# A Fourier-convolution layer with a feed-forward part: first forward stage on 64x64 tiles over two PSUM banks, kernel units finished in pairs, a rebuilt handover and a new order

## The chip, the cores and the metric

The kernel runs on one core of a Trainium2 chip. The metric is the device time in microseconds of one execution; the runs are given with their median. PE is the matrix engine (PEld its weight loads), DVE the vector engine, ACT the scalar engine, POOL the GpSimd engine, SP the engine that issues DMAs. All compute engines run their own instruction streams in order and wait for each other through semaphores.

## The reference

```python
x = A_u                                             # 1 x 2048 x 512
sa, ca, ga, sb, cb, gb = (silu(c) @ w_mod) in six   # each 512 wide
h = layernorm(x) * (1 + ca) + sa
x = x + ga * A(h)
h = layernorm(x) * (1 + cb) + sb
x = x + gb * B(h)

def A(u):          # per channel d of 512, N = 128 complex modes, L = 2048
    K[d, l] = real(sum_n C[d, n] * exp(dt * A[d, n] * l) * dt * B[d, n])
    y = causal convolution of u[:, d] with K[d]     # by FFT of length 2 L
    return y + u * Dskip

def B(x):          # F = 1792
    return relu(x @ w1 + b1) ** 2 @ w2 + b2
```

All data are 32-bit floats.

## The kernel before

Two parts follow each other. The first computes the convolution by a Fourier transform written as matmuls; the second is the feed-forward part, whose matmuls run on values split into a high and a low half (type fp32r).

**The convolution.** The 512 channels are taken in `NC` = 8 blocks of 64, lettered A to H. Sequence positions are split into 32 x 64 points. For a block, `u_pieces` transforms the input: four calls of `stage1` (each: 4 groups of 4 channels, 8 matmuls with 64 columns of data as weights and 128 moving columns of the constant `d1_sb`, into one PSUM bank, and one ACT copy), then four calls of `stage2` (16 matmuls against the table `t2_sb`), copied by ACT. Its fourth piece also copies the halves of the spectrum crosswise by two DMAs (`sws`, `sw`). `d1_sb` is block diagonal in four blocks of 32 rows and columns.

The kernel K is computed in `NU` = 32 units of 16 channels. For unit u, POOL makes the phases (`kgen_phase`, L729) and amplitudes (`kgen_amp`, L749, L753), ACT the sines (L739 to L741), DVE their products (`kgen_rl`, L763 to L766), and PE sums over the modes with 128x32 tiles (`kgen_mm`, L773) into one half of the bank `kg`. `finish(u)` then copies that half to `ksb` (ACT L836), adds the skip term (DVE L837) and calls `stage1` on it. `product_pieces(c)` (letters a to h) runs `stage2` on the block's kernel spectrum, multiplies it on DVE with the input's (L783), and transforms back in a first step (L792, four blocks of 16 matmuls, copied by DVE, L798).

PSUM has eight banks: a ring `ps` of three for stage1, stage2 and L792, one bank `kg`, and four (`tg`) for the sines. The amplitudes lie in a ring of three buffers in `rtl` and `llph`, so POOL's amplitude of unit u waits until PE has used that of unit u - 3.

**What sets the order.** The strings of `ORDER` say which pieces are traced between units u and u + 1 (r rows of the first layernorm, x exponentials, l late modulation, A to H and a to g as above). `keep_order` then reorders: it simulates all engines with the durations of `weight` and takes, per engine, the ready group with the longest way to the end (`urgent` adds to it). The resulting order of each engine is fixed before the run.

**The handover.** The last block's product (`last`) is traced by hand, not by `ORDER`. Meanwhile w1 is split into halves (ACT L897, POOL L918) and w2 partly (ACT L893, POOL L894); `inverse(n)`, n = 0 to 3 (L946, 32x32 tiles, 128 matmuls each into the four `accs` banks), makes the second step of the back transform for a quarter of the rows, which DVE (n = 0) or ACT (L955) evacuates and POOL adds to the input (L958). Four rows of 128 at a time are then normalised: `statistics(s)`, `prepare(s)` (norm on DVE L973, the scaled bias b2 added to x on POOL L975, four transposes L979, scale and shift on ACT L986 and, for s < 4 and q > 1, DVE L982; cast on ACT L990, low half `h0l` on POOL L992).

**The feed-forward part.** 56 rounds of `ffn1` (12 matmuls of 128x512, L1040 to L1043) and `ffn2` (12, L1060 to L1062), PE alone being full. Here PE runs 1344 such matmuls, whatever comes before.

Of the kernel before, what the change touches and what calls it, by code (L numbers as in the profile page):

```python
# [36 lines left out]
NC = 512 // NCH  # L37
# [3 lines left out]
    "rxrrrrrrrrrrrrrrrABAAABDAlAA..DBBA.BD.BDaDBaaDaCCa..xaBaaC.C.CbbDbbCEECb."  # L41
    ".CEbE.b.bcccc.Dcxc..c.HcEEdxdddEdE..G.ddH.deeeeFFH.eHGFFeF..FGFFe.GeGHffGHffGfGf."
    ".H..ff.gg.ggH.gg.gg"
# [58 lines left out]

def weight(ins):
# [3 lines left out]
    if "DMA" in type(ins).__name__:  # L107
# [10 lines left out]
            if cols == 32 and ins.ins[1].ap[0][1] == 32:  # L118
                return 42, 42 + 200
            tiles = 128 // cols if cols in (32, 64, 128) else 1  # L120
# [21 lines left out]
def keep_order(tc, traced, slots, in_turn, whole, urgent):  # L142
# [101 lines left out]
    for _ in groups:  # L244
# [7 lines left out]
        if e == "PE":  # L252
            kind = free_size(groups[g][0].ins[1]) if len(groups[g][0].ins) > 1 else shape
# [38 lines left out]
def tile_adaln_ssm_ffn(  # L292
# [41 lines left out]
    PS, XY = 3, 7  # L334
# [180 lines left out]
    urgent = {}  # L515
# [7 lines left out]
    hurry(mark, 125781)  # L523
# [7 lines left out]
    hurry(mark, 150000)  # L531
# [45 lines left out]
    gs4, g4, s4 = (ctile(n, [P, 128]) for n in ("gs4", "g4", "s4"))  # L577
# [12 lines left out]
    hurry(mark, -13262)  # L590
# [3 lines left out]
    def row_pieces():  # L594
        for s, row in enumerate(rows):
# [10 lines left out]
            hurry(mark, 150000)  # L606
# [11 lines left out]
    def late_modulation():  # L618
        for wm, v in ((wm_sb, sbc), (wm_cb, cbc)):
            m = bank("ps", PS)  # L620
            mod_rows(wm, m)
            mt = ring(kp, "mt", 1, [P, 128])
# [11 lines left out]
    def stage1(src, dst, o):  # L634

        ps = bank("ps", PS)
        for i in range(4):
            for r in range(2):
                nc.tensor.matmul(  # L639
                    ps[64 * r : 64 * r + 64, 128 * i : 128 * i + 128], src[:, i], d1_sb[:, r], start=True, stop=True)  # L640
        nc.scalar.copy(dst[:, o // 4], ps.rearrange("p (t m) -> p m t", t=4))  # L641
# [24 lines left out]
    def u_pieces(c):  # L666
        xs = xus[c] = spectrum()
        for g in range(4):
            stage1(x_sb[c][:, 4 * g : 4 * g + 4], xs, 4 * g)
            yield  # L670
        for g in range(4):
            nc.scalar.copy(piece(xs, g), stage2(xs, g))
            if g == 3:
                sw = sws[c] = spectrum()
                for h in range(2):
                    nc.sync.dma_start(sw[64 * h : 64 * h + 64], xs[64 - 64 * h : 128 - 64 * h])
            yield

# [144 lines left out]
    work.update((chr(97 + c), product_pieces(c)) for c in range(NC - 1))  # L823
# [4 lines left out]
    def finish(u):  # L828

        c = u // 4  # L830
        if u % 4 == 0:
            xks[c] = spectrum()
        kps = kg[:, u % 2]
        kgen_mm(kq.pop(u), kps)
        ksb = ring(kp, "ksb", 2, [P, 4, 64])
        nc.scalar.copy(ksb, kps)  # L836
# [296 lines left out]
```

## Time and profile before

| what | value |
|---|---|
| median of 3 runs | 651.43 us (649.11 to 651.5) |
| the profiled execution | 646.92 us |
| its span | 645.1 us |
| PE, DVE, ACT, POOL busy | 584.7, 384.0, 342.2, 302.7 us |
| mean granted clock of PE | 0.984 |

In a row of instruction groups stand the line, engine, operation, the tiles (out<-in), the shapes, the count, then busy time, mean ns of one, and the idle time just before with what ended it. A 32-bit matmul of the code is two records in the trace. In rows of groups by line and shape, `128*64` is the tile of PE in rows and columns of the array. The digits of the page are busy tenths in 40 slices of 16.1 us.

### The profile page before, as it was taken

The page shows a single profiled execution, that of the slowest core. Times are in us where ns is not written, and L with a number is a line of the kernel's source. Part 1 is how long each engine was busy: PE and PEld are TensorE (multiplying, and loading weights), DVE is VectorE, ACT ScalarE, POOL GpSimd, SP SyncE. Part 2 cuts the span into 40 slices and gives each one's busy share as a digit, 9 for nine tenths or more (in the row PEclk, how much of TensorE's full clock was granted, in tenths as well). Part 3 has the DMA queues.
Part 4 walks back from the last instruction along what each step waited for, and adds up shares of the span by engine and source line. Part 5 has one row for each costly group of instructions (what it writes and reads, how often), then busy time and mean ns, then how long its engine had stood idle before and what let it go on. Part 6 is the DMA issues. An engine that isn't in the chain of part 4 may idle for free.

```text
span 645.1 us, 20810 instructions
## 1 busy us (share of the span) xinstructions
PE 584.7 (91%) x9314; PEld 507.1 (79%) x9314; DVE 384.0 (60%) x655; ACT 342.2 (53%) x632; POOL 302.7 (47%) x243
## 2 busy tenths in 40 slices
PE   1367998999899999987899999999999999999995
PEld 1265997899799998885668888888888888888884
DVE  6999956899799778744659532533325333252223
ACT  5963888989887977361645532244322433222220
POOL 5696799889999887158969300011000100000000
PEclk9999999999999999998799999999999999999998
DMA  9942030311331233465222000100001000010001
GB/s 324 381 133 68 3 69 4 68 36 38 69 70 39 82 69 86 139 206 201 85 83 73 28 0 1 65 1 0 1 1 66 1 1 1 0 66 0 1 1 65
DMA packets 21705, 42.30 MB, mean 66 GB/s; under 512 B 3696, under 2 KB 9200, under 8 KB 20336
## 3 DMA queue, kind: packets, MB, share of 16 engines
q1 hardware_dynamic: 21184, 40.84, 20.8%
q8 instruction: 73, 1.20, 0.8%
q10 hardware_dynamic: 432, 0.14, 0.1%
q14 instruction: 16, 0.13, 0.1%
HBM read 28.39 MB, written 4.19 MB: 51 GB/s over the span
## 4 chain that ended last, share of the span: by engine, by line
PE 71%; DVE 11%; POOL 7%; issue 5%; ACT 4%; DMA 2%; DVEq 0%; SPq 0%; POOLq 0%; ACTq 0%
PE tg L1060 8%; PE tg L1062 8%; PE tg L1061 8%; PE ps L1040 6%; PE ps L1041 6%; PE ps L1043 6%; PE ps L649 6%; PE ps L792 6%; PE ps L639 5%; PE kg L773 3%; PE kg L1040 2%; PE kg L1041 2%; PE kg L1043 2%; ACT tables L720 2%; DVE xy L598 2%
## 5 line engine op out<-in xcount | busy, mean ns | idle before, releaser
L1048 DVE TENSOR_TENSOR xy<-xy 128x512 f32<-128x512 f32 x56 | 44.6, 796 | 157.8 <-ACT rw L1047 106.2
L1046 ACT ACTIVATE xy<-ps,b1c 128x512 f32<-128x512 f32 x42 | 28.9, 688 | 129.7 <-PE ps L1043 129.7
L975 POOL TENSOR_TENSOR big<-big,lo 128x512 f32<-128x512 f32 x16 | 21.6, 1355 | 152.9 <-DVE xy L973 152.5
L649 PE MATMUL ps<-xy,t_sb 128*64 128x64 f32 x2048 | 67.1, 223 | 1.8 <-DVE xy L783 0.9
L649 PEld LDWEIGHTS ps<-xy,t_sb 128*64 128x64 f32 x2048 | 63.9, 138 | 3.8 <-issue 1.1
L792 PE MATMUL ps<-e_sb,xy 128*64 128x128 f32 x1024 | 61.3, 274 | 4.7 <-ACT xy L641 1.9
L792 PEld LDWEIGHTS ps<-e_sb,xy 128*64 128x64 f32 x1024 | 56.0, 139 | 6.3 <-ACT xy L641 2.3
L641 ACT COPY xy<-ps 128x512 f32<-128x512 f32 x64 | 36.8, 589 | 11.8 <-PE ps L639 10.1
L753 POOL TENSOR_TENSOR rtl<-tables 128x1024 f32<-128x1024 f32 x22 | 43.0, 1955 | 0.1
L783 DVE TENSOR_TENSOR xy<-ps,xy 128x512 f32<-128x512 f32 x64 | 40.0, 683 | 2.0 <-PE ps L649 1.7
L798 DVE COPY big<-ps 128x256 f32<-128x256 f32 x64 | 24.2, 419 | 20.3 <-PE ps L792 20.0
L729 POOL TENSOR_TENSOR llph<-lo,big 128x1024 int32<-128x1024 int32 x16 | 34.3, 2141 | 3.8 <-ACT tg L741 2.3
L1040 PE MATMUL ps<-h0h,w1h 128*128 128x512 f32 x88 | 35.8, 407 | 0.0
L729 POOL TENSOR_TENSOR rtl<-lo,big 128x1024 int32<-128x1024 int32 x16 | 34.3, 2141 | 2.8 <-ACT tg L741 2.1
L639 PE MATMUL ps<-d_sb,ksb 128*64 128x128 f32 x512 | 33.2, 274 | 1.1 <-DVE ksb L837 0.6
L639 PE MATMUL ps<-d_sb,big 128*64 128x128 f32 x512 | 31.4, 274 | 0.8 <-ACT big L605 0.7
L1040 PE MATMUL ps<-h,w1h 128*128 128x512 f32 x80 | 31.4, 393 | 0.0
L1046 ACT ACTIVATE xy<-kg,b1c 128x512 f32<-128x512 f32 x14 | 9.6, 689 | 39.4 <-PE kg L1043 39.4
L1049 DVE TENSOR_TENSOR rw<-xy,rw 128x512 fp32r<-128x512 f32 x37 | 28.5, 770 | 2.9
L639 PEld LDWEIGHTS ps<-d_sb,ksb 128*64 128x64 f32 x512 | 28.0, 137 | 2.3 <-DVE ksb L837 1.0
L639 PEld LDWEIGHTS ps<-d_sb,big 128*64 128x64 f32 x512 | 27.9, 137 | 2.0 <-ACT big L605 1.0
L773 PE MATMUL kg<-rtl 128*32 128x64 f32 x1408 | 25.6, 221 | 4.1 <-issue 4.1
(247 smaller groups left out, 1574.0 us busy)
## 6 DMA issues: line engine op xcount, KB each, us to landing
xy<-xt SPq DMA_DIRECT2D x32, 256.0 KB, 5.2
xy<-xy SPq DMA_DIRECT2D x16, 512.0 KB, 6.1
xy<-w_mod SPq DMA_DIRECT2D x6, 1024.0 KB, 8.6
out_dram<-xy SPq DMA_DIRECT2D x16, 256.0 KB, 2.1
xy<-w SPq DMA_DIRECT2D x14, 256.0 KB, 2.7
raw<-w SPq DMA_DIRECT2D x6, 512.0 KB, 5.4
t_sb<-c_t SPq DMA_DIRECT2D x1, 2048.0 KB, 16.9
i2c<-c_i SPq DMA_DIRECT2D x1, 2048.0 KB, 8.7
```

Of the source, the lines that this page charges most:

```text
L639: nc.tensor.matmul(ps[64 * r : 64 * r + 64, 128 * i : 128 * i + 128], src[:, i], d1_sb[:, r], start=True, stop=True)
L649: nc.tensor.matmul(ps[64 * r : 64 * r + 64, 64 * i : 64 * i + 64].rearrange("p (h q t) -> p q h t", h=2, t=2), t2_sb[:, 8 * g + i, r], src ...
L729: nc.gpsimd.tensor_tensor(ph.rearrange("p d r (a b) -> p (d r) a b", a=4), bc(low_phase[:, us].rearrange("p d r b -> p (d r) b"), 2, 4), b ...
L773: nc.tensor.matmul(kps[32 * q : 32 * q + 32, d, :], am[:, r, 4 * q + d, 64:96], am[:, r, 4 * q + d, 0:64], start=(r == 0), stop=(r == 1))
L792: nc.tensor.matmul(ps[64 * m : 64 * m + 64, 128 * i : 128 * i + 128], pairs(y)[:, g, i // 2, 64 * m : 64 * m + 64, i % 2], e1_sb[:, h], st ...
L1040: pe.append(nc.tensor.matmul(ps, w1h[:, q, fs], hh[:, q, :], start=(q == 0), stop=False))
L1041: pe.append(nc.tensor.matmul(ps, wl[:, q], hh[:, q, :], start=False, stop=False))
L1043: pe.append(nc.tensor.matmul(ps, w1h[:, q, fs], hl[:, q, :], start=False, stop=(q == 3)))
L1048: nc.vector.tensor_mul(rr, rr, rr)
L1060: pe.append(nc.tensor.matmul(acc, r2l[:, ms], hi_, start=(t == 0), stop=False))
L1061: pe.append(nc.tensor.matmul(acc, r2h[:, ms], lo_, start=False, stop=False))
L1062: pe.append(nc.tensor.matmul(acc, r2h[:, ms], hi_, start=False, stop=(t == NF - 1)))
```

## The change

Five things change.

1. `stage1` takes 8 groups a call instead of 4, as 32 matmuls on 64x64 tiles: the upper and the lower 64 rows of the data go to two row halves of the array, each with its half of `d1_sb` (the blocks that are zero are left out), and write to two banks, which ACT copies one after the other. The matmul count of stage 1 doubles, the moving columns halve.
2. `finish` copies two units at once from the whole `kg` bank and calls `stage1` once for both.
3. The crosswise DMAs become pieces of their own (digits in `ORDER`), and the last block's product a lettered piece (h).
4. The handover: `inverse(n)` alternates between the `tg` banks and the `ps` and `kg` banks, and inverses 0 and 1 stand in a fixed turn on PE; for s < 4 the norm runs on ACT instead of DVE, three of four scale-and-shift steps on DVE instead of two, and the scaled bias is made and added after the inverses.
5. `ORDER`, the `hurry` values and the planner's PE costs are new. A few small tiles (`gs4`, `g4`, `s4`, `mt`) move into buffers that are free by then.

```diff
+def shape_of(ins):
+    return free_size(ins.ins[1]) + 1000 * (ins.ins[1].ap[0][1] == 64)
...
+            if cols == 64 and rows == 64:
+                return 30, 30 + 170
...
-    hurry(mark, 125781)
+    hurry(mark, 107010)
...
-        hurry(mark, 7656)
+        hurry(mark, 36379)
...
     def stage1(src, dst, o):
 
-        ps = bank("ps", PS)
-        for i in range(4):
-            for r in range(2):
-                nc.tensor.matmul(
-                    ps[64 * r : 64 * r + 64, 128 * i : 128 * i + 128], src[:, i], d1_sb[:, r], start=True, stop=True)
-        nc.scalar.copy(dst[:, o // 4], ps.rearrange("p (t m) -> p m t", t=4))
+        banks = [bank("ps", PS) for _ in range(2)]
+        for i in range(8):
+            for r, h in ((0, 0), (1, 1), (1, 0), (0, 1)):
+                hs = slice(64 * h, 64 * h + 64)
+                m = nc.tensor.matmul(
+                    banks[h][64 * r : 64 * r + 64, 64 * i : 64 * i + 64], src[hs, i], d1_sb[hs, r, hs], start=True, stop=True)
+                whole[m.ins.name] = banks[0].tensor.name
+        for h, ps in enumerate(banks):
+            nc.scalar.copy(dst[:, 2 * o : 2 * o + 2, 64 * h : 64 * h + 64], ps.rearrange("p (d t m) -> p d m t", d=2, t=4))
...
+    def swap_piece(c):
+        xs, sw = xus[c], spectrum()
+        sws[c] = sw
+        for h in range(2):
+            nc.sync.dma_start(sw[64 * h : 64 * h + 64], xs[64 - 64 * h : 128 - 64 * h])
+        yield
...
     def finish(u):
 
-        c = u // 4
-        if u % 4 == 0:
+        kgen_mm(kq.pop(u), kg[:, u % 2])
+        if u % 2 == 0:
+            return
+        c, o = u // 4, u // 2 % 2
+        if o == 0:
             xks[c] = spectrum()
-        kps = kg[:, u % 2]
-        kgen_mm(kq.pop(u), kps)
-        ksb = ring(kp, "ksb", 2, [P, 4, 64])
-        nc.scalar.copy(ksb, kps)
-        nc.vector.tensor_add(ksb[:, :, 63], kps[:, :, 63], ds4[:, 4 * u : 4 * u + 4])
-        stage1(ksb, xks[c], 4 * (u % 4))
+        ksb = ring(kp, "ksb", KSB, [P, 8, 64])
+        both = kg.rearrange("p u d x -> p (u d) x")
+        nc.scalar.copy(ksb, both)
+        nc.vector.tensor_add(ksb[:, :, 63], both[:, :, 63], ds4[:, 4 * u - 4 : 4 * u + 4])
+        stage1(ksb, xks[c], o)
...
-        banks = [t.rearrange("p (i c d) -> p i c d", i=4, c=NC) for t in accs]
+        banks = [t.rearrange("p (i c d) -> p i c d", i=4, c=NC) for t in (accs if n % 2 == 0 else tb)]
...
+        if n < 2:
+            in_turn.update(i for i, w in whole.items() if w.startswith("inverse"))
...
-        nc.vector.tensor_scalar(
-            d4(xn), x2[:, s], mv[:, s, 0:1], rstd2[:, s : s + 1], op0=ALU.subtract, op1=ALU.mult)
-        nc.gpsimd.tensor_add(x2[:, s], x2[:, s], d4(b2g))
+        if s < 4:
+            nc.vector.scalar_tensor_tensor(
+                mv[:, s, 1:2], mv[:, s, 0:1], -1.0, rstd2[:, s : s + 1], op0=ALU.mult, op1=ALU.mult)
+            nc.scalar.activation(d4(xn), x2[:, s], AF.Identity, scale=rstd2[:, s : s + 1], bias=mv[:, s, 1:2])
+        else:
+            nc.vector.tensor_scalar(
+                d4(xn), x2[:, s], mv[:, s, 0:1], rstd2[:, s : s + 1], op0=ALU.subtract, op1=ALU.mult)
+        if s > 3:
+            nc.gpsimd.tensor_add(x2[:, s], x2[:, s], d4(b2g))
...
     inverse(2)
     inverse(3)
+    nc.sync.dma_start(b2g, b2.partition_broadcast(P))
+    nc.gpsimd.tensor_mul(b2g, gbb, b2g)
+    for s in range(4):
+        nc.gpsimd.tensor_add(x2[:, s], x2[:, s], d4(b2g))
```

Line numbers shift: L639 becomes L647, L649 L659, L773 L786, L792 L805, L946 L955, L918 L927, L894 L905, L975 for s < 4 L1035, L958 L969, L992 L1009, L505 L512, L729 L742, L749 L762, L753 L766.

**PE in the first kernel units, before.** The big tile is the input, ksb a finished unit, kg a kernel unit, t_sb the stage-2 table; the last number counts the matmuls.

```order
L639 MATMUL ps_152<-d_sb,big_84 64x128 x8
L649 MATMUL ps_150<-xy_97,t_sb 64x16x2x2 x16
L639 MATMUL ps_151<-d_sb,ksb_959 64x128 x8
L773 MATMUL kg_351<-rtl 32x64 x32
L639 MATMUL ps_150<-d_sb,big_84 64x128 x8
L649 MATMUL ps_152<-xy_91,t_sb 64x16x2x2 x16
L639 MATMUL ps_151<-d_sb,ksb_960 64x128 x8
```

And the same place of the change, with the middle of the 32 stage-1 matmuls left out:

```order
L659 MATMUL ps_152<-xy_97,t_sb 64x16x2x2 x16
L786 MATMUL kg_348<-llph 32x64 x32
L647 MATMUL ps_150<-d_sb,ksb_1039 64x64
L647 MATMUL ps_151<-d_sb,ksb_1039 64x64
...
L659 MATMUL ps_152<-xy_91,t_sb 64x16x2x2 x16
L659 MATMUL ps_150<-xy_91,t_sb 64x16x2x2 x16
```

A stage-1 call now alternates between two banks of the ring and stands once for two units; each unit's kg block stands alone.

**POOL at the start of the unit work, before**, where the rows of the first layernorm are on DVE. L505 and L501 are steps on the parameters of blocks B to H, L753 and L729 unit work.

```order
L729 TENSOR_TENSOR rtl<-lo,big_83 128x1024
L723 TENSOR_TENSOR tables_370<-tables_370,big_83 128x64x4
L753 TENSOR_TENSOR rtl<-tables_370 128x16x64
L729 TENSOR_TENSOR llph<-lo,big_83 128x1024
L497 TENSOR_TENSOR big_83<-big_83 128x7x64
...
L723 TENSOR_TENSOR tables_371<-tables_371,big_83 128x64x4 x2
L505 TENSOR_TENSOR big_83<-big_83 128x7x64
L501 TENSOR_TENSOR big_83<-big_83 128x7x64
```

Of the change:

```order
L742 TENSOR_TENSOR rtl<-lo,big_83 128x1024
L512 TENSOR_TENSOR big_83<-big_83 128x7x64
L504 TENSOR_TENSOR big_83<-big_83 128x7x64
...
L736 TENSOR_TENSOR tables_368<-tables_368,big_83 128x64x4 x2
L508 TENSOR_TENSOR big_83<-big_83 128x7x64
```

The step L505, now L512, moved ahead of the unit work; L501, now L508, stayed behind it.

**POOL in the handover, before**: w1 and w2 splits, the four bias adds (L975), then the low halves h0l (L992) with adds of the input (L958) between them.

```order
L753 TENSOR_TENSOR rtl<-tables_371 128x16x64
L918 TENSOR_TENSOR w1la<-raw_4100,w1h 128x4x256
L882 COPY i2c<-xy_92 128x1
...
L894 TENSOR_TENSOR w_5005<-xy_93,w_5005 128x512 x3
L975 TENSOR_TENSOR big_83<-big_83,lo 128x4x8x16 x4
L992 TENSOR_TENSOR h0l<-xy_91,h0h 128x4x128
L958 TENSOR_TENSOR big_83<-big_83,xy_92 128x4x8x16 x3
L992 TENSOR_TENSOR h0l<-xy_91,h0h 128x4x128 x3
```

Of the change:

```order
L766 TENSOR_TENSOR rtl<-tables_368 128x16x64
L895 COPY i2c<-xy_95 128x1
L927 TENSOR_TENSOR w1lb<-raw_4545,w1h 128x4x256
...
L1035 TENSOR_TENSOR big_83<-big_83,lo 128x4x8x16 x2
L969 TENSOR_TENSOR big_83<-big_83,xy_94 128x4x8x16 x2
L905 TENSOR_TENSOR w_5479<-xy_91,w_5479 128x512
L1009 TENSOR_TENSOR h0l<-xy_92,h0h 128x4x128 x4
```

The first split now writes w1lb, which lies where the stage-2 table lay, instead of w1la; three bias adds and two adds of the input stand ahead of the four h0l steps.

More of the change, by code (lines that the diff above doesn't have):

```diff
@@ L897, in tile_adaln_ssm_ffn @@
         nc.scalar.copy(w1h[:, :, f : f + n], raw1[f // 896][:, :, f % 896 : f % 896 + n])
[L898 to L901 removed]
+    nc.scalar.activation(rings["ksb"][0][(NU // 2 - 1) % KSB][:, 0, 0:1], epsb, AF.Sqrt)
     nd, nx, nk = (spectra[i].tensor.name for i in (2, 3, 4))
```

49 lines of the change are left out of this document (20 added, 29 removed).

## The prediction

> **What bounds the kernel now.** I read the page first, then the busy times by stage, then the waits and the chain inside the stages that the change touches. The page:
>
> ```profile
> span 645.1 us, 20810 instructions
> PE 584.7 (91%) x9314; PEld 507.1 (79%) x9314; DVE 384.0 (60%) x655; ACT 342.2 (53%) x632; POOL 302.7 (47%) x243
> PE   1367998999899999987899999999999999999995
> POOL 5696799889999887158969300011000100000000
> ```
>
> PE is busy almost everywhere, but its last half is one dense stage that the change leaves alone. POOL's digits are the second thing to see: 8s and 9s from slice 8 to slice 15. The stages, cut where the last row piece, the last kernel unit, the last convolution block and the first feed-forward matmul lie:
>
> ```profile
> core 0: us, PE busy (x) PEld busy (x) DVE busy (x) ACT busy (x) POOL busy (x), PEclk, DMA share, GB/s
> 63.50:80.00 16.50, 16.09 (x456) 15.00 (x458) 14.90 (x25) 13.82 (x21) 12.11 (x7) 1.00 0.01 3
> 80.00:260.00 180.00, 171.35 (x4984) 162.50 (x4980) 147.99 (x234) 153.02 (x245) 163.20 (x119) 1.00 0.24 56
> 260.00:295.60 35.60, 31.94 (x820) 30.45 (x817) 20.04 (x41) 14.33 (x22) 14.62 (x11) 1.00 0.67 206
> 295.60:320.50 24.90, 18.20 (x785) 13.77 (x785) 14.57 (x36) 11.23 (x27) 22.51 (x17) 0.73 0.33 105
> 320.50:338.50 18.00, 16.97 (x307) 12.79 (x305) 9.15 (x22) 9.78 (x22) 11.63 (x10) 0.91 0.30 89
> 338.50:638.00 299.50, 299.50 (x1345) 248.01 (x1344) 117.50 (x171) 99.88 (x177) 32.34 (x22) 1.00 0.05 16
> ```
>
> From 63.5 to 295.6 (the convolution) PE works 219.4 of 232.1 us, so it idles only 12.7. POOL is close behind: 163.2 of 180. From 338.5 to 638.0 PE never stops. So there are two places where time can come from: PE work in the convolution, and the 42.9 us between convolution and dense stage, where POOL is the busy one (22.51 of 24.90). How far POOL follows a faster PE is in its waits between 80 and 262 us:
>
> ```profile
> POOL rtl L749 <- PE kg L773: 9.6, 7, 2.7
> POOL rtl L729 <- ACT tg L741: 2.1, 2, 1.6
> POOL llph L729 <- DVE llph L764: 1.6, 1, 1.6
> POOL rtl L749 <- DVE rtl L764: 1.3, 1, 1.3
> ```
>
> Two thirds of POOL's waiting is for PE to release an amplitude buffer. Without any wait POOL would be done some 15 us earlier, not more.
>
> **Stage 1 on PE.** The chain, where nothing but PE is on it, gives the price of each block (start, length, what):
>
> ```profile
> 134.57 1.05 PE kg L773 x64
> 135.63 1.90 PE ps L792 x32
> 137.53 1.75 PE ps L639 x32
> 139.28 0.93 PE ps L649 x32
> ```
>
> The records are twice the matmuls of the code, so 32 records of L639 are two calls of stage1, at 0.875 us each. There are 64 calls:
>
> ```profile
> L639 PE MATMUL ps<-d_sb,ksb 128*64 128x128 f32 x512 | 33.2, 274 | 1.1 <-DVE ksb L837 0.6 <-ACT xy L641 0.4
> L639 PE MATMUL ps<-d_sb,big 128*64 128x128 f32 x512 | 31.4, 274 | 0.8 <-ACT big L605 0.7
> ```
>
> 64 x 0.875 = 56.0 us. After the change a call does twice as much, in 64 records on four 64x64 tiles with 64 moving columns, 32 calls in all. No block of this shape is in the trace. Nearest is the kernel unit (L773): also 64 records, also four tiles, also 64 moving columns, 1.05 us, 16.4 ns a record. It differs in that its four tiles lie in four column groups; the new ones lie in two column groups and two row halves. So the question is whether two row halves run side by side. If not, a record costs what L649 pays, which has 64 moving columns on two column groups: 0.93 / 32 = 29 ns, and a call 1.86 us. The inverse has row groups, in this stretch at half clock:
>
> ```profile
> core 0: us, PE busy (x) PEld busy (x), PEclk, DMA share, GB/s
> 309.60:311.20 1.60, 1.52 (x64) 0.95 (x64) 0.50 0.56 164
> ```
>
> Sixty-four records of 64 moving columns on a 4 by 4 grid. Were only the column groups to overlap, each would hold 16 records of 2 x 29 = 58 ns, twice that at half clock: 1.86 us. It took 1.52 with its drain, so row groups overlap at least in part. I take 1.05 us, the row it is nearest to, and keep 1.86 as the other end. Sum: 32 x 1.05 = 33.6, a gain of 22.4 us of PE time.
>
> [...]
>
> Changes of tile shape cost something: L792 takes 1.90 right behind L773 and 1.75 elsewhere, 0.15 more. In PE's order the 64- or 32-column blocks entered from another shape number 63 before; in the new order 34 + 29 of the old shapes are, and the 30 entries into the new shape are within the 1.05. So nothing is added.
>
> **Units in pairs.** Evacuations:
>
> ```profile
> L641 ACT COPY xy<-ps 128x512 f32<-128x512 f32 x64 | 36.8, 589 | 11.8 <-PE ps L639 10.1 <-DVE xy L783 1.6
> L836 ACT COPY ksb<-kg 128x256 f32<-128x256 f32 x32 | 11.9, 371 | 12.6 <-PE kg L773 12.5
> L837 DVE TENSOR_TENSOR ksb<-kg,ds 128x4 f32<-128x4 f32 x32 | 5.1, 160 | 8.7 <-ACT ksb L836 8.5
> ```
>
> Stage 1's copies stay 64 of 128x512. The 32 of ksb become 16 of 589 ns: ACT saves 11.9 - 9.4 = 2.5 us, DVE 16 x 0.16 = 2.6. Neither ends a wait by itself; I count nothing. What is added is a hold: a call now owns two of the three ps banks until ACT has copied both (2 x 0.589, one after the other). PE's next block that needs a bank waits for that, and everything queued behind it on PE; that is the slower rival below. The swaps (digits in the order) are the same two 512 KB DMAs a channel, on the same SP queue, behind their last piece; the weight loads queued behind them there are not wanted before the handover. Nothing.
>
> **The order, and where the convolution ends.** POOL's start and end:
>
> ```profile
> 62.01 1.33 POOL L505 TENSOR_TENSOR big<-big 128x448 int32<-128x448 int32 x1 [4.67 <-DVE big L473]
> 258.15 1.95 POOL L753 TENSOR_TENSOR rtl<-tables 128x1024 f32<-128x1024 f32 x1
> 281.09 2.38 POOL L918 TENSOR_TENSOR w1la<-raw,w1h 128x1024 fp32r<-128x1024 f32 x1 [20.98 <-PE ps L792]
> ```
>
> L505 waited 4.67 us for a DVE step queued behind the rows; in the new order that DVE step stands before them. The next POOL step still needs DVE work after the rows, so of the 4.67 I take 2.5. Of the 14.6 us of waits above I let 6 go: PE is faster, but it still has other work in front of the units. So POOL's last unit step ends at 260.1 - 2.5 - 6 = 251.6. What follows it now takes 35.5 us, since PE is behind. In the new order PE has behind the last pair of units (2 x 1.05) two stage-1 calls, eight L792 blocks and four L649 blocks, 2.1 + 14.0 + 3.7, and the small gb block, 0.5: 22.4 in all, and about 4 for DVE's four products of the last unit and the copies: 26.5. The convolution ends at 278.1 instead of 295.6: 17.5 us gained. PE's own sum allows it: 219.4 - 22.4 + 12.7 = 209.7 us from 63.5, that is 273.2; so 5 us of new waits are in my number. Bounds: with all POOL waits gone 10 more; with none gone and a tail of 30 us, 8 gained.
>
> **The handover.** POOL, whose rows are:
>
> ```profile
> L918 POOL TENSOR_TENSOR w1lb<-raw,w1h 128x1024 fp32r<-128x1024 f32 x3 | 7.2, 2385 | 0.0
> 300.08 1.28 POOL L918 TENSOR_TENSOR w1lb<-raw,w1h 128x512 fp32r<-128x512 f32 x1
> L894 POOL TENSOR_TENSOR w<-xy,w 128x512 fp32r<-128x512 f32 x6 | 7.6, 1284 | 2.4 <-ACT w L893 2.4
> L975 POOL TENSOR_TENSOR big<-big,lo 128x512 f32<-128x512 f32 x16 | 21.6, 1355 | 152.9 <-DVE xy L973 152.5
> L958 POOL TENSOR_TENSOR big<-big,xy 128x512 f32<-128x512 f32 x12 | 16.5, 1398 | 6.4 <-ACT big L955 6.4
> L992 POOL TENSOR_TENSOR h0l<-xy,h0h 128x512 fp32r<-128x512 f32 x4 | 5.2, 1326 | 0.0
> ```
>
> In the new order the first weight split writes where the stage-2 table lay, so POOL starts after the last L649, five L792 blocks before the end E of the convolution: about E - 10 (now it starts at 281.09, E - 14.5). Up to the last h0l there stand 6 x 2.385 + 2 x 1.28 (w1 splits), 7.6 (w2), 1.28 (the bias row), three L975-like adds 4.1, two L958-like 2.8, and 5.2: 37.8. So h0l is complete at E + 28, and the first feed-forward matmuls, whose first eight do not need it (8 x 0.223 = 1.8), can run without a gap from E + 26. PE's own way there: both last inverses now stand before them, and ACT must empty inverse 3's banks first; I take E + 28. Today they start at E + 24.9, but then lose 18.0 - 48 x 0.223 = 7.3 us up to 338.5 to inverses, waits and half clock, so they count as starting at E + 32. Gain 4; bounds 0 and 7. The moved norm (ACT instead of DVE, 4 x about 0.6) and the alternate banks lie within this. From there on PE has the same 300 us.
>
> **The sum.** The profiled execution took 646.9, 1.8 beside its span. 646.9 - 17.5 - 4 = 625.4. The runs have a median of 651.4, 4.5 above it; so 629.9, forecast 630.
>
> **Rivals.** (1) POOL and ACT hold the convolution: POOL keeps its waits, 8 us gained there, nothing at the handover: 643. For it: POOL busy 91% in the longest stage. Against: 9.6 of its waits are PE's. (2) Records of this shape do not pass as fast as L773's: the row halves overlap only in part, and a record takes 23 ns, midway between 16.4 and 29. A call is then 1.45 us, PE gains 32 x 0.30 = 9.6, and with the handover's 4 it ends at 638. For it: the inverse's 1.52 shows overlap in part, no more. [...] (3) The row halves do not overlap: stage 1 costs 32 x 1.86 = 59.5, 3.5 more; with the handover's 4 it ends at 651. Against it the inverse's 1.52. (4) Slower: the two banks. ACT runs its queue in order, and sine steps of over 1 us stand between its copies; if PE waits at each call 1 us for a bank, 32 us come back, against 22.4: 9.6 - 4 = 5.6 slower, 657. It decides from (22.4 + 4) / 32 = 0.83 us a call. Against it: now PE waits for ACT's stage-1 copies only this much from 63 to 296 us:
>
> ```profile
> PE ps L792 <- ACT xy L641: 1.9, 2, 1.3
> ```
>
> For it: with one free bank instead of two the cover is thinner.
>
> **Chances.** Forecast 0.67, (1) 0.12, (2) 0.06, (3) 0.04, (4) 0.11. A measurement of this kernel tells about 0.5%, 3 us, from no change. Faster is the forecast, (1) and (2): 0.85; same (3): 0.04; slower (4): 0.11. The range: 630 less 10 when all POOL waits go, to (1) with a little room: 620 to 645; (3), (4) and a tail of the forecast, under 0.2, lie outside.
>
> **What would show it.** Stage-1 blocks of 64 records at 1.0 to 1.1 us (right), about 1.45 (rival 2) or 1.86 (rival 3). The last convolution block's end near 278, PE's idle time before it near 18 us, POOL's last unit step near 252. PE waits on ACT's stage-1 copies summing to over 20 us would be rival 4. The dense stage without a gap from about 306, 300 us long; if it starts late with POOL's h0l as the releaser, the handover term is wrong. A dense stage that got longer would make the whole working wrong.

## The result, and the profile after

The changed kernel takes 666.06 us (median of 4 runs, 663.35 to 669.88) against 650.27 us for the kernel before in the same comparison: a ratio of 1.0255, with a 95% interval of 1.0213 to 1.0296. It is slower, where 630 us and faster was forecast. The profiled execution took 666.28 us, with a span of 664.5. Medians and ratios below leave out one execution, of a later kernel, that ran in a slower state of the chip.

The page of the changed kernel (the q8 line is from its part on DMA queues: packets, MB, share of 16 engines' span):

```profile
span 664.5 us, 22853 instructions
PE 577.2 (87%) x10338; PEld 497.2 (75%) x10338; DVE 378.0 (57%) x643; ACT 342.6 (52%) x616; POOL 301.9 (45%) x243
PE   1367778879997889699679999999999999999995
PEclk9999999989998899899779999999999999999998
q8 instruction: 81, 1.33, 0.8%
```

PE's busy time fell, from 584.7 to 577.2 us, and still the span is 19.4 us longer. PE's digits, 9s and a few 8s from slice 5 to slice 18 before, hold four 7s, three 8s and a 6, and the granted clock has four 8s from slice 9 to slice 17, where before it had none ahead of the handover. The q8 line was not read in the prediction. The same line of the kernel before, and PE's clock there:

```profile
PEclk9999999999999999998799999999999999999998
q8 instruction: 73, 1.20, 0.8%
```

The new stages, cut at the end of the last back-transform block (L805) and at the first feed-forward matmul:

```profile
core 0: us, PE busy (x) PEld busy (x) DVE busy (x) ACT busy (x) POOL busy (x), PEclk, DMA share, GB/s
63.50:313.00 249.50, 211.53 (x7286) 196.88 (x7277) 179.10 (x280) 179.63 (x271) 185.85 (x131) 0.96 0.29 77
313.00:344.40 31.40, 22.15 (x1040) 16.88 (x1040) 17.60 (x44) 15.59 (x34) 29.32 (x23) 0.76 0.26 74
344.40:658.00 313.60, 313.42 (x1392) 258.79 (x1392) 122.26 (x190) 107.52 (x192) 40.38 (x29) 0.99 0.06 20
```

The convolution ends at 312.8 instead of the forecast 278.1. PE is idle for 38.0 us of it (12.7 before, 18 forecast) at a mean clock of 0.96 (1.00 before). From there to the end it takes 351.7 us, where it took 350.1 before, from the end of the last back-transform block (L792) at 295.0. So nearly all of the loss is in the convolution. What PE waits for there, between 63 and 313 us (total, times, longest):

```profile
PE kg L786 <- issue: 11.7, 7, 3.1
PE ps L647 <- issue: 6.3, 4, 3.3
PE ps L805 <- issue: 6.0, 3, 3.9
PE ps L659 <- issue: 5.7, 9, 1.2
PE ps L647 <- ACT xy L651: 1.5, 2, 0.9
PE ps L805 <- ACT xy L651: 1.4, 1, 1.4
PE ps L659 <- ACT xy L651: 1.2, 1, 1.2
```

29.7 us are "issue": time in which PE waited for no other engine, no semaphore and no DMA that the kernel issues. Waits for the stage-1 copies are 4.1 us, so the slower rival of the two banks is not it. Before, in the same stage, issue was 4.8 us:

```profile
PE kg L773 <- issue: 4.1, 3, 2.0
PE ps L649 <- issue: 0.7, 1, 0.7
```

Where these waits lie is seen in PE's timeline (start, busy, records, and in brackets the idle time ahead):

```profile
74.53 0.75 PE L786 MATMUL kg<-rtl 128*32 128x64 f32 x35 [0.84 <-issue]
75.21 1.16 PE L647 MATMUL ps<-d_sb,big 64*64 64x64 f32 x64
76.30 1.09 PE L659 MATMUL ps<-xy,t_sb 128*64 128x64 f32 x29
78.26 0.33 PE L659 MATMUL ps<-xy,t_sb 128*64 128x64 f32 x3 [0.87 <-issue]
79.20 1.13 PE L786 MATMUL kg<-llph 128*32 128x64 f32 x64 [0.61 <-DVE ksb L853]
80.25 1.15 PE L647 MATMUL ps<-d_sb,ksb 64*64 64x64 f32 x60
82.62 0.33 PE L647 MATMUL ps<-d_sb,ksb 64*64 64x64 f32 x4 [1.22 <-issue]
```

Count the records from one issue wait to the next: 35 + 64 + 29 = 128, then 3 + 64 + 60 = 127, the weight load of the next one, and a semaphore instruction of PE's queue (at 79.09), which counts as well. They stop in the middle of a stage-2 block and of a stage-1 block, whatever the line. A record is one weight load and one matmul (the page counts 10338 of each), two instructions, so these stops of PE lie 256 instructions apart. That is also what the q8 line counts: 81 packets of 16 KB (1.33 MB), and 81 x 256 = 20736 against 2 x 10338 = 20676 instructions in PE's records; before 73 packets for 2 x 9314. **PE waits for its own instructions**, which come by DMA in blocks of 256.

The times of the q8 packets in the trace confirm it. Each of the 57 blocks that begin in the changed convolution begins at least 1.2 us after the packet of its own number has landed, and the 23 of them that begin with a stop of over 0.5 us begin 1.2 to 1.6 us after it. At 82.62, for example, PE goes on 1.36 us after a packet that began at 80.31 and took 0.95 us.

For a ledger I went through PE's instructions in the trace, from the first stage-1 record to the last back-transform record. Gaps are counted from one start to the next, so they come out somewhat longer than PE's idle time in the profile. "At block starts" sums them at every 256th instruction; "other gaps" are those over 0.4 us elsewhere; of the stretches at half clock half counts as lost, which is an estimate; "work" is what is left of the length. In us:

| kernel | length | at block starts | other gaps | at half clock | work |
|---|---|---|---|---|---|
| before | 231.3 | 6.4 | 9.2 | 0 | 215.6 |
| after | 248.0 | 36.3 | 8.7 | 20.5 | 192.8 |

The work fell by 22.8 us, where 22.4 were forecast. Block starts took 29.9 back and the half clock 10.2.

With the long waits the granted clock fell too. In the rows below PE waits 3.27 us for a block, while a crosswise swap of two 512 KB DMAs is under way (DMA share 0.44), and then runs at a mean clock of 0.60: 64 L805 records take 5.79 us, where 32 elsewhere take 1.97.

```profile
146.28 1.55 PE L647 MATMUL ps<-d_sb,ksb 64*64 64x64 f32 x44 [3.27 <-issue]
147.76 5.79 PE L805 MATMUL ps<-e_sb,xy 128*64 128x128 f32 x64
157.92 1.97 PE L805 MATMUL ps<-e_sb,xy 128*64 128x128 f32 x32
```

```profile
142.40:146.30 3.90, 0.63 (x26) 0.45 (x23) 3.61 (x5) 1.22 (x2) 3.90 (x4) 0.86 0.44 105
146.30:153.50 7.20, 7.20 (x111) 6.91 (x111) 1.35 (x3) 4.10 (x5) 3.55 (x2) 0.60 0.01 2
```

The last two rows, with the columns of the stages above, are the wait and what follows it. The packet of this block was not slow but late: it took 1.10 us, as others do, but began 4.56 us after the start of the block before, where the median of the 23 stops is 1.2 us. All four waits of over 2.8 us are of this kind; their packets began 3.3 to 4.6 us after the block before.

### The profile page after: what moved, and what is told of

Read it like the earlier page. It is cut to its first block, busy times and chain, and to the rows that moved or that the text cites. A ratio compares the mean times of both kernels' runs of the same rounds, so it can differ in the third digit from the quotient of the medians.

```text
span 664.5 us, 22853 instructions
## 1 busy us (share of the span) xinstructions
PE 577.2 (87%) x10338; PEld 497.2 (75%) x10338; DVE 378.0 (57%) x643; ACT 342.6 (52%) x616; POOL 301.9 (45%) x243
## 3 DMA queue, kind: packets, MB, share of 16 engines
q1 hardware_dynamic: 21184, 40.84, 20.3%
q8 instruction: 81, 1.33, 0.8%
## 4 chain that ended last, share of the span: by engine, by line
PE 74%; DVE 9%; issue 6%; POOL 6%; ACT 4%; DMA 1%; DVEq 0%; POOLq 0%; ACTq 0%
PE ps L659 9%; PE tg L1081 8%; PE tg L1079 8%; PE tg L1080 8%; PE ps L805 7%; PE ps L1059 6%; PE ps L1060 6%; PE ps L1062 6%; PE ps L647 5%; PE kg L786 4%; PE kg L1059 2%; PE kg L1062 2%; PE kg L1060 2%; DVE xy L605 2%; DVE xy L604 1%
## 5 line engine op out<-in xcount | busy, mean ns | idle before, releaser
L1067 DVE TENSOR_TENSOR xy<-xy 128x512 f32<-128x512 f32 x56 | 41.2, 736 | 160.1 <-ACT rw L1066 104.6
L992 POOL TENSOR_TENSOR big<-big,lo 128x512 f32<-128x512 f32 x12 | 16.2, 1350 | 158.0 <-DVE xy L989 158.0
L659 PE MATMUL ps<-xy,t_sb 128*64 128x64 f32 x2048 | 70.2, 226 | 8.1 <-issue 5.7
L659 PEld LDWEIGHTS ps<-xy,t_sb 128*64 128x64 f32 x2048 | 66.0, 141 | 11.2 <-issue 7.5
L805 PE MATMUL ps<-e_sb,xy 128*64 128x128 f32 x1024 | 66.6, 287 | 8.0 <-issue 6.0
L805 PEld LDWEIGHTS ps<-e_sb,xy 128*64 128x64 f32 x1024 | 60.4, 147 | 10.2 <-issue 6.6
L651 ACT COPY xy<-ps 128x512 f32<-128x512 f32 x64 | 34.3, 591 | 26.7 <-PE ps L647 26.5
L766 POOL TENSOR_TENSOR rtl<-tables 128x1024 f32<-128x1024 f32 x22 | 43.1, 1960 | 0.2
L742 POOL TENSOR_TENSOR llph<-lo,big 128x1024 int32<-128x1024 int32 x16 | 34.3, 2145 | 6.6 <-ACT tg L754 6.6
L786 PE MATMUL kg<-rtl 128*32 128x64 f32 x1408 | 27.3, 224 | 11.0 <-issue 10.9
L742 POOL TENSOR_TENSOR rtl<-lo,big 128x1024 int32<-128x1024 int32 x16 | 34.3, 2141 | 5.2 <-ACT tg L754 4.6
L786 PEld LDWEIGHTS kg<-rtl 128*32 128x32 f32 x1408 | 22.9, 111 | 13.6 <-issue 12.4
L762 POOL TENSOR_TENSOR rtl<-tables 128x512 f32<-128x512 f32 x22 | 23.5, 1071 | 17.4 <-PE kg L786 17.4
L777 DVE TENSOR_TENSOR rtl<-rtl,tg 128x1024 f32<-128x1024 f32 x22 | 26.7, 1212 | 1.2 <-POOL rtl L766 1.1
L779 DVE TENSOR_TENSOR rtl<-rtl,tg 128x1024 f32<-128x1024 f32 x22 | 26.7, 1211 | 0.0
```

The source lines that it names most:

```text
L659: nc.tensor.matmul(ps[64 * r : 64 * r + 64, 64 * i : 64 * i + 64].rearrange("p (h q t) -> p q h t", h=2, t=2), t2_sb[:, 8 * g + i, r], src ...
L742: nc.gpsimd.tensor_tensor(ph.rearrange("p d r (a b) -> p (d r) a b", a=4), bc(low_phase[:, us].rearrange("p d r b -> p (d r) b"), 2, 4), b ...
L766: nc.gpsimd.tensor_mul(am[:, 0, :, 32:96].rearrange("p d (v x) -> p d v x", v=2), bc(et[:, 256 + 8 * d0 : 384 + 8 * d0].rearrange("p (y a) ...
L786: nc.tensor.matmul(kps[32 * q : 32 * q + 32, d, :], am[:, r, 4 * q + d, 64:96], am[:, r, 4 * q + d, 0:64], start=(r == 0), stop=(r == 1))
L805: nc.tensor.matmul(ps[64 * m : 64 * m + 64, 128 * i : 128 * i + 128], pairs(y)[:, g, i // 2, 64 * m : 64 * m + 64, i % 2], e1_sb[:, h], st ...
L1067: nc.vector.tensor_mul(rr, rr, rr)
```

## The experiments

Theory A is that PE waits for blocks of its instructions. Theory B is that something else of the change costs the time: the order, the pairs, the handover, or the tiles and copies themselves.

**Old tiles in the new kernel.** Everything else as in the changed kernel, in the same order of every engine; only the layout of the two ACT copies follows the tiles.

```diff
-            for r, h in ((0, 0), (1, 1), (1, 0), (0, 1)):
-                hs = slice(64 * h, 64 * h + 64)
-                m = nc.tensor.matmul(
-                    banks[h][64 * r : 64 * r + 64, 64 * i : 64 * i + 64], src[hs, i], d1_sb[hs, r, hs], start=True, stop=True)
+            for r in range(2):
+                m = nc.tensor.matmul(
+                    banks[i // 4][64 * r : 64 * r + 64, 128 * (i % 4) : 128 * (i % 4) + 128], src[:, i], d1_sb[:, r], start=True, stop=True)
```

> The changed kernel with stage 1 back on 128x64 tiles (16 matmuls of 128 moving columns a call instead of 32 of 64); pairs, handover and the order of every engine stay as in the changed kernel. PE gets 32 x (1.75 - 0.95) = 26 us more matmul work and 2048 instructions less. Theory A (PE waits for its own instructions, which come in blocks of 256, one per about 3.7 us): stalls at the block boundaries in the convolution fall from 24 us to under 10 and the half-clock stretches vanish, so the added work is paid back: 650 to 663 us. Theory B (the new order, the pairs or the handover cost the time): the waits stay and the work comes on top: 680 to 692 us.

Measured: 653.17 us, ratio to before 1.0019 (0.9991 to 1.0047). The work rose by 19.9 us, to 212.7, and the kernel became 13 us faster: the gaps at block starts fell from 36.3 to 12.4 us, the half clock from 20.5 to 6.8. Its page counts 73 instruction packets again. The time is theory A's, and far from theory B's 680; block starts and half clock fell, but not to the under 10 and the nothing that were expected. It also says that the rest of the change (pairs, handover, order) is worth under half a percent either way on these tiles.

**More instructions in the kernel before.** Each stage-1 matmul is split in two of half the columns, with PE's order unchanged.

```diff
-            for r in range(2):
-                nc.tensor.matmul(
-                    ps[64 * r : 64 * r + 64, 128 * i : 128 * i + 128], src[:, i], d1_sb[:, r], start=True, stop=True)
+            for h in range(2):
+                for r in range(2):
+                    m = nc.tensor.matmul(
+                        ps[64 * r : 64 * r + 64, 128 * i + 64 * h : 128 * i + 64 * h + 64], src[:, i],
+                        d1_sb[:, r, 64 * h : 64 * h + 64], start=True, stop=True)
```

> The kernel before with every stage-1 matmul split into two of 64 moving columns on the same 128x64 tile, in the same order on every engine: 2048 more PE instructions, about 64 x 0.055 = 3.5 us more PE work. Theory A (instruction blocks): besides the 3.5 us, stalls at block boundaries grow by 5 to 18 us: 659 to 672 us. Theory B: 653 to 655 us.

Measured: 667.53 us, ratio 1.0243 (1.0150 to 1.0337). Work 219.8 (4.2 more), block starts 20.3 (13.9 more), 6.8 at half clock. The total and the block starts are theory A's. The kernel before, given as many PE instructions as the changed one, is about as slow as the changed one, as far as an interval this wide can say.

**New tiles alone in the kernel before.** Calls of four groups, so each call takes two banks for half the work. The planner makes a new order of every engine for it.

```diff
-        ps = bank("ps", PS)
+        banks = [bank("ps", PS) for _ in range(2)]
...
-        nc.scalar.copy(dst[:, o // 4], ps.rearrange("p (t m) -> p m t", t=4))
+        for h, ps in enumerate(banks):
+            nc.scalar.copy(dst[:, o // 4, 64 * h : 64 * h + 64], ps[:, 0:256].rearrange("p (t m) -> p m t", t=4))
```

> The kernel before with nothing but stage 1 on 64x64 tiles (4 groups a call, two banks half filled, two copies of 256 columns). Theory A (instruction blocks): 26 us of PE work go and most of it comes back as stalls at block boundaries and half clock: 638 to 668 us, with over 15 us of such stalls in the convolution. Theory B (order, pairs or handover to blame): 624 to 632 us.

Measured: 702.09 us, ratio 1.0761 (1.0693 to 1.0828), slower than either theory said. The work is 194.6, so the tiles do pay. Block starts cost 18.8 us, but other gaps rose to 51.7 and the half clock to 37.5 us. PE's waits in its convolution, up to 313 us, name the ACT copies of stage 1 (here L646):

```profile
PE ps L654 <- ACT xy L646: 11.9, 7, 5.7
PE ps L642 <- ACT xy L646: 10.5, 15, 1.4
PE ps L797 <- ACT xy L646: 3.1, 4, 1.3
```

That is the prediction's slower rival, a call that holds two of three banks until ACT has emptied both. With 64 calls it costs 25.5 us in these rows; with the changed kernel's 32 it cost 4.1. This run therefore does not separate A from B by its time. It is a reason to pair the units, which halves their calls; but the order is another one too, so the run does not show what the number of calls alone costs.

**Small swaps.** The changed kernel without most of the crosswise transfer.

```diff
-            nc.sync.dma_start(sw[64 * h : 64 * h + 64], xs[64 - 64 * h : 128 - 64 * h])
+            nc.sync.dma_start(sw[64 * h : 64 * h + 64, 0, 0:32], xs[64 - 64 * h : 128 - 64 * h, 0, 0:32])
```

> The changed kernel with the crosswise DMAs cut to 1/16 of their columns (the rest of the swapped spectrum is left out); the PE order is the same row for row. Theory A with contention (a fetch that queues behind 1 MB of such a transfer comes 3 us late): the four stalls of over 2.8 us lose three of their number, and the half-clock stretches behind them go: 648 to 658 us. Theory A without contention, or theory B: 664 to 668 us.

Measured: 657.83 us, ratio 1.0104 (1.0042 to 1.0166), 8 us below the changed kernel. Block starts fell from 36.3 to 28.3 us, the half clock from 20.5 to 10.2, and the convolution became 12.8 us shorter; 4.9 us of that were lost behind it, for a reason that stays open. One wait of over 2.8 us is left, as expected, but two of 2.7 stand beside it, and three stretches at half clock. So part of the waiting is the swaps' traffic, and three quarters of the block starts' cost stay without it. Other traffic may have a share in these: before two of the three long waits left, at 211 to 216 and 265 to 269.5 us, other DMAs move 1.39 and 1.58 MB.

**The block rate by itself.** Streams of matmuls with no other engine in their way.

> Not the layer: nothing but streams of 32-bit matmuls on constant data (its output is not the reference's). 1536 matmuls on 128x32 tiles with 64 moving columns, the same again with two 512 KB on-chip DMAs every 384 of them, then 128x64 tiles with 128 and with 64 columns, then full 128x128 tiles with 128 and with 64 columns. Theory A: in the first stream PE works 1.9 us and stands still about 1.8 at every 256th instruction, 3.5 to 3.8 us a block, however long it goes on; a block that meets the DMAs takes 6 to 7 us; 128x64 tiles with 128 columns run 7.0 us a block without a stall. Theory B: no stall at any block. The full tile: 112 ns a record with 128 columns, as the gb block of the kernel before shows; with 64 columns 56 to 112.

Its timeline, on 128x32 tiles without DMAs (first rows), and where it meets the first pair of DMAs (last row):

```profile
35.68 1.99 PE L338 MATMUL kps<-x,w 128*32 128x64 f32 x128 [1.71 <-issue]
39.41 1.99 PE L338 MATMUL kps<-x,w 128*32 128x64 f32 x128 [1.74 <-issue]
42.87 1.99 PE L338 MATMUL kps<-x,w 128*32 128x64 f32 x128 [1.46 <-issue]
...
115.79 0.66 PE L338 MATMUL kps<-x,w 128*32 128x64 f32 x33 [1.74 <-issue]
...
124.89 1.99 PE L338 MATMUL kps<-x,w 128*32 128x64 f32 x128 [3.29 <-issue]
```

128 records in 1.99 us, then a stop, again and again: 22 blocks from 35.68 to 115.79, 3.64 us each. By the DMAs the stop grows to 3.29 us; at three of the four pairs such a block takes 5.1 to 5.7 us, less than the 6 to 7 expected, and at the fourth nothing is seen. The q8 packets divide a block's 3.64 us: by the medians of the stops, a packet begins 1.1 us after the start of the block before and takes 1.0 us, and PE goes on 1.4 us after it has landed. Beside the three pairs it begins 2.9 to 3.4 us after. With more columns the same count of instructions takes longer to run, and the stops are gone:

```profile
209.65 84.06 PE L343 MATMUL ups<-x,w 128*64 128x128 f32 x1536
293.54 44.97 PE L343 MATMUL vps<-x,w 128*64 128x64 f32 x1536
```

1536 records are 12 blocks: 7.0 us each with 128 columns, 3.75 with 64, the second just about the block rate. So, by the stream's rate, the changed convolution, whose 14582 PE instructions are 57 blocks, needs 57 x 3.64 = 207 us for them, more than its 192.8 us of work. The one before has 49 blocks, 178 us, below its 215.6 of work. The bound has changed from matmul work to instructions; the 207 us are reached only if no dense stretch ever runs ahead of its blocks.

**Half of the calls.** New tiles for the input side only, and for the kernel units only, in the changed kernel's PE order (the first one shown; the second has `!=`).

```diff
+        if src.tensor.name[:3] == "ksb":
+            for i in range(8):
+                for r in range(2):
+                    m = nc.tensor.matmul(
+                        banks[i // 4][64 * r : 64 * r + 64, 128 * (i % 4) : 128 * (i % 4) + 128], src[:, i], d1_sb[:, r], start=True, stop=True)
...
+            return
```

> The changed kernel with 64x64 tiles only where stage 1 transforms the input (16 calls); the 16 calls on kernel units use 128x64 tiles. Same order on PE: 1024 PE instructions less than the changed kernel, about 10 us more matmul work. Theory A: the 53 blocks need 193 us at 3.64 us each, the matmul work about 203, so neither leads by much: gaps at block starts 18 to 27 us, between the 12 and the 36 of the two ends, total 650 to 660 us. If waiting falls faster than work rises, below 650, which would beat both kernels.

> The other half: 64x64 tiles only where stage 1 transforms kernel units, which PE reaches straight behind the dense blocks of the units themselves. Same count of instructions as with the input side. Theory A: as many blocks, but the dense stretches lie closer together, so gaps at block starts are 2 to 8 us more than with the input side, total 652 to 664 us. If only the count matters, the two are within 2 us.

Measured: 657.1 us (1.0110, 1.0077 to 1.0144) and 654.26 us (1.0063, 1.0035 to 1.0091). Work 202.7 and 203.3, block starts 23.2 and 19.0, half clock 13.7 and 17.1. With 0, 16, 32 new calls the sum of block starts and lost clock is 15.8, 30.1 or 27.6, and 46.5 us, while the work falls by 10 each time: in these traces every step costs more than it brings. In times the first step is clear with the input's side alone; with the units' side alone the interval overlaps that of the old tiles. Both totals lie in their ranges. The guess that the units' side bunches worse was wrong; whether the two sides differ at all is not clear, since their intervals overlap too. Neither beats the kernel before.

**Fewer instructions elsewhere.** The first step of the back transform, and then stage 2 too, with one matmul of 128 weight columns in place of two of 64.

```diff
-                    for m in range(2):
-                        nc.tensor.matmul(
-                            ps[64 * m : 64 * m + 64, 128 * i : 128 * i + 128],
-                            pairs(y)[:, g, i // 2, 64 * m : 64 * m + 64, i % 2],
-                            e1_sb[:, h], start=(h == 0), stop=(h == 1))
+                    nc.tensor.matmul(
+                        ps[:, 128 * i : 128 * i + 128], pairs(y)[:, g, i // 2, :, i % 2],
+                        e1_sb[:, h], start=(h == 0), stop=(h == 1))
```

> The changed kernel with the first step of the back transform (L805) on the full array: one matmul with 128 weight columns in place of two with 64, 1024 PE instructions less, 1.79 instead of 1.75 us a block of work. Theory A: four blocks of 256 less to fetch, 8 to 14 us gained: 650 to 660 us. Theory B: nothing gained, 665 to 668 us.

Measured: 656.22 us, ratio 1.0104 (1.0073 to 1.0135): 10 us below the changed kernel, inside theory A's range. Block starts 24.5, half clock 6.8 us; work 199.4, which is 6.6 us more than the changed kernel's, not 1.3: a block of L805 takes 2.08 us to the start of what follows, 1.90 in the changed kernel. The planner moved some groups for it, so not all of the 10 us need be instructions.

> The changed kernel with stage 2 (L659) on the full array as well, in the same PE order: 3072 PE instructions less in the convolution. Theory A, if a full-tile record of 64 columns costs 56 to 60 ns: the stalls at block boundaries and the half clock go, and the 26 us of stage 1 come through: 628 to 645 us, faster than both kernels. If that record costs 112 ns, stage 2 gets 64 x 0.86 = 55 us longer: 690 us or more. Theory B, at 56 to 60 ns: 665 to 668 us.

> The kernel before with both steps (L792 and L649) on the full array, 3072 PE instructions less. Theory A, at 56 to 60 ns a record: the 4.8 us of stalls at block boundaries in its convolution and some hidden ones go, the matmul work stays: 642 to 649 us. At 112 ns: 690 us or more. Theory B: 650 to 653 us.

Measured: 695.11 us (1.0736, 1.0670 to 1.0803) and 704.88 us (1.0849, 1.0809 to 1.0889), the case of the expensive record. The stream kernel has its price, 128 and 64 columns together (each 512 records):

```profile
338.44 114.56 PE L358 MATMUL wps<-x,w 128*128 128x128 f32 x1024
```

112 ns a record, and each 128 records take 14.3 us in either half: 64 columns cost as much as 128. Two 128x64 tiles side by side pass two records of 64 columns in 2 x 29 ns (the 44.97 us for 1536 above), so stage 2 is better left on them.

> The kernel before with only its first step of the back transform (L792) on the full array: 1024 PE instructions less, 32 x 0.04 = 1.3 us more matmul work, order planned anew. Theory A: up to 5 us of stalls go, 645 to 651 us. Theory B: 650 to 654 us.

Measured: 653.59 us, ratio 1.0037 (1.0015 to 1.0058). That is theory B's range. Block starts fell from 6.4 to 2.2 us, as theory A says, but the work rose by 11.2, to 226.8: no gain. Fewer blocks bring little where blocks do not bind.

**An order that knows of blocks.** The planner of `keep_order` was given a rule: PE may cross into a block no earlier than 3.64 us after it crossed into the one before, and a group that would wait for a block ranks lower (in the control this second part has the weight 0). `ORDER` and the `hurry` values were searched again with it, for the changed kernel with the full-tile back transform, and as a control for the kernel before. The changed kernel on its own tiles has no measured run with such an order.

```diff
+        if (n + k) // 256 > n // 256:
+            start = max(now, fetched)
+            cost += start - now
+            now = start
+            fetched = start + FETCH
```

> The same planner and search for the changed kernel with the first step of the back transform on the full array (1024 PE instructions less). Theory A: 638 to 648 us, at best faster than both kernels by 1%; theory B: no better than the 656 us of the full tile alone.

> A control: the kernel before with the same planner and as long a search. Its convolution needs 49 blocks of 3.64 us, 178 of its 231 us, so there is little to win by counting them. Theory A: 645 to 653 us. If the search by itself is worth something, 640 us or less.

Measured: 669.5 us (1.0265, 1.0220 to 1.0309) and 654.7 us (1.0060, 1.0036 to 1.0085). The first is a miss, slower than both theories said: block starts are 22.5 us, hardly below the 24.5 without the search, other gaps 17.8 and the half clock 23.9. A constant 3.64 us knows nothing of swaps that make a block late, nor of the clock; that this is the reason is a guess. The control lies just above theory A's range and shows that the search alone brings nothing. That a better order could save part of the waiting stays possible; it is not shown.

**The handover.** Half of the inverses' matmuls left out.

```diff
-            for r in range(2):
+            for r in range(1):
```

> The changed kernel with half of the inverses' matmuls (the sine terms are left out): 1024 PE instructions less between the convolution's end and the dense part, where the changed kernel takes 351.6 us from the last L805 to the end. If PE's instruction blocks hold that part, it gets 4 to 9 us shorter: total 656 to 662 us. If POOL's row up to h0l sets it (28.5 us behind the last L805, as forecast), it stays within 2 us: 664 to 668 us.

Measured: 658.65 us, ratio 1.0114 (1.0065 to 1.0163). From the end of the last L805 to the end it takes 342.3 us, 9.4 less. That is the time of the reading by PE's blocks, but the run does not show its cause. The planner also gave POOL another row: four of the six w2 steps and two of the three adds of the scaled bias moved behind h0l, and two more adds of the input ahead of it.

```profile
304.52 2.38 POOL L927 TENSOR_TENSOR w1lb<-raw,w1h 128x1024 fp32r<-128x1024 f32 x1 [23.95 <-PE ps L659]
332.82 3.73 POOL L1009 TENSOR_TENSOR h0l<-xy,h0h 128x512 fp32r<-128x512 f32 x3 [0.80 <-ACT h0h L1007]
337.25 0.80 PE L1059 MATMUL ps<-h0h,w1h 128*128 128x512 f32 x1 [0.66 <-ACT big L966]
```

From its first w1 split to the end of h0l POOL takes 32.0 us with 0.8 us of waiting; in the changed kernel it took 38.5. So 6.5 of the 9.4 us can as well be POOL's shorter row, and the run does not separate the two readings.

## Why the prediction was wrong

The step that failed is the one under "The order, and where the convolution ends": "5 us of new waits are in my number". PE's idle time was taken to rise from 12.7 to about 18 us because PE's matmul sum allowed it. By the same measure it was 38.0 us, and 20.5 us of the stretch ran at half clock, for which the prediction had no term; that costs another 10.2. These 20 us more of idle time and the 10 of lost clock make 30 of the 34.7 us by which the convolution ended late. What PE waited for was blocks of its own instructions. The issue waits, 4.8 us before, do not occur in the prediction. It doubled stage 1's matmul count, priced each record, and did not ask at what rate PE gets its instructions.

- **Stage 1 on PE**: right in the price. A call is 64 records in 1.16 us with its drain (the row at 75.21), 1.09 to the start of what follows, and 22.8 us of work went, 22.4 forecast. That close an agreement is partly luck: against the old tiles in the same order the work is 19.9 us less, and 2.9 come with the rest of the change. The row halves overlap; rivals 2 and 3, with 1.45 and 1.86 us a call, fall. A record of 64 columns on four tiles in turn costs much the same in the bare stream: its rows give 1.99 us for 128 records, drain included, 15.5 ns each.
- **Changes of tile shape at nothing**: not quite. In the same order a call takes 1.80 us with the old tiles and 1.09 with the new, so 32 calls save 22.7 us, of which the work shows 19.9; a block of L805 took 1.80 us with the old and 1.90 with the new. For full tiles it fails: there the work rose by 6.6 us.
- **POOL**: its last unit step was forecast to end at 251.6. It ended at 272.2 (the row of L766 below). POOL's waits for PE to release an amplitude buffer grew from 9.6 to 17.4 us instead of falling. From there to the end of the convolution 26.5 us were forecast and 40.6 measured; in these PE stands 3.86 and 1.61 us at block starts and runs 6.8 us at half clock. The small gb block in it takes 1.2 us (8 records), not the 0.5 that the sum has.

```profile
POOL rtl L762 <- PE kg L786: 17.4, 8, 3.6
270.25 1.96 POOL L766 TENSOR_TENSOR rtl<-tables 128x1024 f32<-128x1024 f32 x1
302.91 2.39 POOL L927 TENSOR_TENSOR w1lb<-raw,w1h 128x1024 fp32r<-128x1024 f32 x1 [24.25 <-PE ps L659]
```

- **Handover**: POOL's sum was right: h0l was complete at 341.4, 28.6 us behind the convolution's end, 28 forecast. But the first feed-forward matmul came only at 344.4, 31.6 behind the convolution's end, after ACT's evacuation of the last inverse (L966), and the next ones ran at half clock (0.50 from 344.4 to 350.0). On the chain that ended last this evacuation stands behind an ACT step on the row statistics, and that behind POOL's add that follows h0l; the forecast had counted POOL's row only up to h0l. The stretch to the end is 1.6 us longer than before, not 4 shorter.

```profile
336.24 5.15 POOL L1009 TENSOR_TENSOR h0l<-xy,h0h 128x512 fp32r<-128x512 f32 x4
344.40 0.80 PE L1059 MATMUL ps<-h0h,w1h 128*128 128x512 f32 x1 [0.27 <-ACT big L966]
```

- **Rival 4, the two banks**: its mechanism exists (25.5 us with 64 calls in another order), but costs little in the changed kernel (4.1 us). The kernel became slower for a reason that no rival named.
- **The dense stage**: as forecast, without a gap once it runs (313.42 of 313.60 us busy); its start comes late with everything before it.

The forecast 214.6 us for 63.5 to 278.1 and the block rate collide at once: 57 blocks in it leave 3.76 us a block, 0.12 over what a stream with nothing else beside it gets.

## What to carry to other kernels

Before a matmul is split into smaller tiles, count PE's instructions, four for each 32-bit matmul, and set them against the rate at which blocks of 256 arrive: here 3.64 us a block in the bare stream, 14 ns an instruction. In the changed convolution 23 of 57 blocks began with a stop of over 0.5 us, with no other engine to wait for. Look for "issue" waits that come every 128 records in the profile of before; even a few microseconds of them say that the rate is near, and that cheaper records may buy waits. In the changed kernel the four waits of over 2.8 us came with 20.5 us at half clock, and in the stream, beside two 512 KB DMAs, a block came late three times of four.

## What the runs showed of the hardware

- PE's instructions arrive in blocks of 256, one per 3.64 us in a stream that needs nothing else; beside two 512 KB DMAs a stop of 1.5 to 2.0 us grew to 3.1 to 3.7, three times of four.
- In that stream the packet of a block began 1.1 us after the block before, took 1.0 us, and PE went on 1.4 us after it had landed. Where a block was over 2.8 us late in the changed convolution, its packet began late (3.3 to 4.6 us) and was as quick as others.
- Two row halves of the array on 64x64 tiles run side by side: 64 records in 1.16 us, where 1.86 was the estimate without overlap.
- A 32-bit record on the full array took 112 ns with 64 columns as with 128 (14.3 us for 128 records).
- With each of the four waits of 2.8 to 3.9 us in the changed convolution the granted clock stood at 0.50 for 3.4 or 6.8 us. Three of these stretches began 0.4 to 1.1 us before PE went on, one 1.0 us after. The length of the wait alone did not decide: with the new tiles on the units alone a wait of 2.0 us was followed by half clock, with the full-tile back transform one of 2.85 us was not, and in the bare stream the 128 records behind the stop of 3.29 us took 1.99 us, as elsewhere.
